# Retention and two feed-forward layers: keys loaded earlier, outputs ahead of scores, weight steps denser

## The chip, the cores and the metric

The kernel runs on one core of a Trainium2 chip. The metric is the device time of one execution in microseconds. TensorE (PE) multiplies matrices, VectorE (DVE) and ScalarE (ACT) do elementwise work and read the results out of PSUM, GpSimd (POOL) does elementwise work in SBUF, and SyncE (SP) issues every transfer, one after the other from one queue.

## The reference

The attention-like part has no softmax: scores are weighted by a decay that depends on the distance of the positions and on the head. Its output, 2304 tokens by 512, goes through two feed-forward layers one after the other, each with its own weights (512 by 2048 and 2048 by 512). All of it is float32.

```python
B, H, S, D = 4, 8, 576, 64
scores = scale * q @ k.transpose(0, 1, 3, 2)
gamma = 1 - 2.0 ** (-5 - arange(H))
ret = scores * where(rel >= 0, gamma ** rel, 0)   # rel = query position - key position
x = (ret @ v) as (B*S, H*D)

h = x @ w_in;  x = maximum(0.01 * h, h) @ w_out   # first layer
h = maximum(x @ w2_in, 0);  out = (h * h) @ w2_out   # second layer
```

## The kernel before

**Retention.** Each batch's 576 positions are cut into four chunks of 128 and one of 64, so there are 20 chunks, counted from 0. For chunk i `load` fetches transposed queries and keys (256 KB each), `load_rows` keys and values by rows (512 KB together), `load_gq` a decay table in the first batch. `scores(i)` forms all heads' scores on TensorE in one of the two big PSUM tiles (a for even, b for odd chunks), and VectorE multiplies them by the decay mask into r (line 513); so the scores of chunk i+2 wait until r of chunk i is done. `decay(i)` scales queries and keys in place on GpSimd (lines 522, 526). `output(i)` multiplies r by the values (line 539), adds the decayed query times the state (line 542), adds this chunk to the state sums (line 548), and ScalarE copies the state (line 554) and the output into ysb (line 557). `keep_warm(n)` issues n products of a zero tile whose result is not used (line 466).

**Weights.** Products run in float32 split into a high and a low part of a format that TensorE takes faster. Weights come from memory in a raw form, 1 MB (two transfers of 512 KB) a task, through a single buffer (the first task through ysb's last tile). A task is a generator of steps: twelve for the first matrix (`steps_in`: lines 149 to 187), eight for the second (`steps_out`: lines 149 and 201 to 216); each step is one to four instructions. Group 0 has four tasks, two of each kind, 40 steps; the sixth step of a second-matrix task, or the seventh of a first-matrix one, asks for the next task's load. During retention that request only sets `free`, and the chunk loop issues the load at its next turn; after retention the load is issued at once, and the task's steps may start only `ARRIVE` units of the planner's clock later. `RATE[i]` says how many steps follow chunk i's output, `OWN` how many of the 40 are left for later, `FIRST` how many run before the loop.

**Operands.** As soon as 768 tokens are out, `operands` builds seven sums and differences of their blocks, each as x with a high part by ScalarE (line 256) and a low part by VectorE (line 260), one step a chunk (`BUILD`). They are stored to memory for later groups (line 237 in the profile).

**Products.** The first matrix is multiplied by a seven-product scheme (`first`), in the order A11, A12, S2, S3, S1, A22, S4. A11, S2, S1 and S4 add into PSUM tile a, A12 into b; S3 starts b anew and A22 adds to it. So t (line 370, from A11 and A12) must have read b before S3, the copy s of S3 (line 344) must be done before A22, and t22 (line 384) must have read a before S4. `second` then multiplies by the second matrix (yps, line 419). There are four groups of weights a layer and three blocks of 768 tokens a group. A11 and A12 of the first block, and S2 behind them, stand among the last two chunks. `pace` runs weight and operand steps between products: at most two weight steps a call, by planned shares. It also issues the stores of x.

Every engine takes its instructions in the order in which the program was written; there is no other scheduler.

Of the kernel before, what the change touches and what calls it, by code (L numbers as in the profile page):

```python
# [23 lines left out]
GRP = 4  # L24
# [6 lines left out]
HW = DM // 2  # L31
SLOTS = 7
INS, OUTS = 3, 2 * NU
RATE = [1, 2, 2, 2] + [2] * 6 + [1, 1, 2, 2, 2, 0, 0, 0, 1, 2]
BUILD = [0] * 8 + [1] * 11 + [0]
DEEP = 4
SPACE = .65
SHARE = {0: (0.15, 0.45), NG - 1: (0.47, 0.85), NG: (0.2, 0.55)}
OWN = 5
LAG = 1  # L40
ARRIVE = 3
FIRST = 3
AHEAD = 2
WARM = 10, 3, 1
BIGGEST = float(np.uint32(0x0FEFFFFF).view(np.float32))

A22, A11, A12, S1, S2, S3, S4 = range(7)
# [3 lines left out]
def retention_ffn_kernel(ctx: ExitStack, tc: tile.TileContext, full, rows, half, halfv, w1, w2, const, mask, gk, out):  # L51
# [54 lines left out]
    class Weights:  # L106
# [30 lines left out]
        def next(self):  # L137

            if self.later:
                self.free = not self.raws  # L140
            else:
                self.ahead()
# [99 lines left out]
    def operands(layer, p):  # L242

        x = ysb[p].rearrange("p (k t n) -> p k t n", k=NK, t=2)
        b11, b21, b12, b22 = (x[:, k : k + 2, t] for t in range(2) for k in (0, 2))
        t2 = stage.tile([P, 2, HT], F32, tag="t2", name="t2")

        xt = {}

        def hi(i, src):  # L250
            use = layer, 0, p, i
            while uses[loaded[0]] != use or loaded[0] == used[0] + SLOTS:
                yield True
            loaded[0] += 1
            xt[i] = xs[use] = xpool.tile([P, 2, 2, HT], F32R, tag="x", name="x")
            nc.scalar.activation(xt[i][:, 0], src, AF.Copy)

        def lo(i, src):
            t = xt[i]
            nc.vector.tensor_tensor(t[:, 1], src, f32(t[:, 0]), sub)  # L260
            kept.append(((layer, 0, p, i), t))


        yield from hi(0, b11)
        yield
        yield from hi(1, b21)
        lo(0, b11)
        yield
        lo(1, b21)
        nc.vector.tensor_tensor(b11, b12, b11, sub)  # L270
        yield
        nc.vector.tensor_tensor(t2, b22, b11, sub)
        yield
        yield from hi(2, t2)
        nc.vector.tensor_tensor(b12, b22, b12, sub)
        yield
        yield from hi(3, b12)
        lo(2, t2)
        yield
        yield from hi(4, b11)  # L280
        nc.vector.tensor_tensor(b21, b21, t2, sub)
        yield
        yield from hi(5, b21)
        lo(3, b12)
        yield
        yield from hi(6, b22)
        lo(4, b11)
        yield
        lo(5, b21)
        yield  # L290
        lo(6, b22)
        yield
# [152 lines left out]
    def tokens(i):  # L445
        b, c = chunks[i]
        return b * S + c * P, P if c < FULL else S - FULL * P
# [112 lines left out]
    weights = Weights()  # L560
# [5 lines left out]
    def run(n, limit):  # L566

        while n > 0 and done[0] < limit:
            if next(steps, None):
                break  # L570
            done[0] += 1
            n -= 1
# [13 lines left out]
    GROUP = NU * (STEPS_IN + STEPS_OUT)  # L586
    with tc.manual_schedule():
        with tc.tile_pool(name="att", bufs=1) as pool:
            att.append(Retention(pool))
            ret = att[0]  # L590
            n = len(chunks)
            ret.load(0)
            ret.load_mask()
            ret.load_rows(0)
            ret.load_gk()
            weights.ahead()
            ret.load(1)
            ret.load_rows(1)
            ret.load_gq(1)
            ret.load(2)  # L600
            ret.load_rows(2)
            ret.load_gq(2)
            ret.load(3)
            ret.load_rows(3)
            ret.load_gq(3)
            ret.keep_warm(WARM[0])
            ret.scores(0)
            ret.decay(0)
            run(FIRST, GROUP)
            scored = 1  # L610
            for i in range(n):
                if i + DEEP < n:
                    ret.load(i + DEEP)
                    ret.load_rows(i + DEEP)
                    if i + DEEP <= FULL:
                        ret.load_gq(i + DEEP)
                if weights.loads < GRP and (weights.free or i == 1):
                    weights.free = False
                    weights.ahead()

                while scored < n and scored <= i + (AHEAD if i > 2 else min(i, 1)):
                    ret.scores(scored)
                    ret.decay(scored)
                    scored += 1
                ret.keep_warm(WARM[i + 1] if i + 1 < len(WARM) else 0)
                ret.output(i)
                a, t = tokens(i)
                if a < 2 * HT <= a + t:
                    builds.append(operands(0, 0))
                run(min(1, RATE[i]), GROUP - OWN)  # L630
                if BUILD[i] > 0:
                    build()
                run(RATE[i] - 1, GROUP - OWN)
                if BUILD[i] > 1:
                    build()
                if i >= n - 3 and i < n - 1:

                    early.append(wide(i - n + 3))
                    product(early[-1], [wt_in[0, 0], wt_in[0, 2]], (A11, A12)[i - n + 3], uses[i - n + 3], True)
                    if i == n - 3:  # L640
                        sums1 = stage.tile([P, NU, HT], F32, tag="t2", name="s")
                        nc.scalar.activation(sums1, early[0][:, :, :HT], AF.Copy)
                    else:
                        early.append(sums1)
        att.clear()
        if weights.free and weights.loads < GRP:
            weights.ahead()
        more = ctx.enter_context(tc.tile_pool(name="more", bufs=1))
        gp = ctx.enter_context(tc.tile_pool(name="gp", bufs=1))
        weight_tiles(more, INS - NU, OUTS - NU)  # L650
        run(GROUP, GROUP - OWN)
        weights.arrive = ARRIVE
        weights.later = False


        whole = NB * 15
        for layer in range(2):
            for g in range(NG):
                i = layer * NG + g


                start = i * GROUP + GROUP
                limit = start + (GROUP if i < 2 * NG - 1 else 0)

                def pace(now, ceiling):

                    into = min(1, (now - 15 * p) / (6 if busy[p] else 12 if p == NB - 1 else 15))
                    share = (0, *SHARE.get(i, (0.36, 0.71)), 1)
                    part = share[p] + (share[p + 1] - share[p]) * into
                    want = start + math.ceil((limit - start) * part)  # L670

                    while len(kept) > LAG:
                        store(*kept.pop(0))
                    while builds and now >= built[0] and build():
                        built[0] = max(built[0], now - 1) + SPACE
                    if not builds:
                        while kept:
                            store(*kept.pop(0))
                    weights.clock = whole * i + now
                    if now % 15 not in (6, 8):  # L680
                        run(min(2, max(want, start if now > 1 else 0) - done[0]), ceiling)

                busy = [g == 0] * (NB - 1) + [layer == 0 and g == NG - 1]
                for p in range(NB):
                    built = [15 * p + 8]
                    if g == 0 and p + 1 < NB:
                        builds.append(operands(layer, p + 1))
                    elif layer == 0 and g == NG - 1 and p == NB - 1:
                        builds.append(operands(1, 0))

                    def in_first(m):
                        if i == p == m == 0:
                            return
                        pace(15 * p + m + 1, max(start, limit - 3))

                    def in_second(t, j, part):

                        if t or j or part in (0.5, 1):
                            pace(15 * p + 7 + 4 * t + 2 * (j + part), limit if p == NB - 1 else max(start, limit - 3))
                        load_x()  # L700

                    gs = first(layer, g, p, in_first)
                    second(layer, g, p, gs, in_second)
                    build(99)
                weights.due = 0
                run(GROUP, limit)
# [56 lines left out]
```

## Time and profile before

| | |
|---|---|
| three runs | 845.59 us median (843.33 to 846.24) |
| profiled execution | 844.29 us, of which the span is 842.50 us |
| mean granted clock of TensorE | 0.993 of full speed |
| TensorE busy | 824.2 us (98%), VectorE 601.4 (71%), ScalarE 340.7 (40%), GpSimd 49.8 (6%) |

The span is what the trace covers, from the first instruction to the last. Times in rows count from its start. Retention takes roughly the first 88 us of it; the rest is the two layers. Engine names in rows: PE, PEld (its weight loads), DVE, ACT, POOL, SPq (SyncE's issue of a transfer).

### The profile page before, as it was taken

To read this page: it belongs to the slowest core of one execution; us is meant where nothing else is said; L and a number is where in the kernel's file an instruction comes from. 1 tells how busy PE (TensorE), PEld (TensorE's weight loads), DVE (VectorE), ACT (ScalarE), POOL (GpSimd) and SP (SyncE) were. 2 spreads that over 40 slices of the span, in tenths; PEclk is the share of its full clock that TensorE was granted. 3 is DMA by queue.
4 is the path that set the end of the run, shared out by engine and by line. 5 is a ranking of instruction groups with operands and counts; after the bars stand their busy time and mean duration, and the time that the engine had idled before them with its cause. 6 is when DMAs were issued, how large, how long until landed. Compare 5 with 4: busy or idle time off the path is not lost.

```text
span 842.5 us, 12378 instructions
## 1 busy us (share of the span) xinstructions
PE 824.2 (98%) x5084; PEld 778.0 (92%) x5084; DVE 601.4 (71%) x734; ACT 340.7 (40%) x447; POOL 49.8 (6%) x36
## 2 busy tenths in 40 slices
PE   6999999999999999999999999999999999999998
PEld 6878899999999999999999998988998998998996
DVE  4799588758667576658667879868777778754534
ACT  1455557545424424424425365543322333321211
POOL 3766000000000000000000000000000000000000
PEclk8999999999999999999999999999999999999999
DMA  9998463967547647646832554966755646735711
GB/s 334 346 311 288 181 241 95 420 264 279 217 190 268 219 150 298 242 147 242 301 112 103 209 226 163 368 255 238 285 183 206 262 160 252 262 133 204 286 52 75
DMA packets 45688, 191.01 MB, mean 227 GB/s; under 512 B 5696, under 2 KB 6720, under 8 KB 45632
## 3 DMA queue, kind: packets, MB, share of 16 engines
q1 hardware_dynamic: 45632, 190.22, 60.7%
q8 instruction: 40, 0.66, 0.3%
q14 instruction: 16, 0.13, 0.0%
HBM read 152.45 MB, written 37.75 MB: 226 GB/s over the span
## 4 chain that ended last, share of the span: by engine, by line
PE 86%; DVE 7%; DMA 4%; ACT 1%; issue 1%; SPq 0%; DVEq 0%; ACTq 0%
PE yps L419 46%; PE a L318 22%; PE b L318 16%; DMA raw<-in_w 1%; DVE r L513 1%; DMA x<-x 1%; DVE x L260 1%; PE scps L511 1%; DMA kt<-in_full 1%; DMA kv<-in_rows 1%; PE ops L539 1%; PE ops L542 1%; DVE sf L205 1%; ACT sf L149 1%; DVE ilo L187 1%
## 5 line engine op out<-in xcount | busy, mean ns | idle before, releaser
L318 PE MATMUL a<-x,ihi 128*128 128x384 f32 x768 | 196.0, 336 | 2.2 <-DVE t L384 2.1
L318 PE MATMUL b<-x,ihi 128*128 128x384 f32 x576 | 147.2, 336 | 2.1 <-DVE t L370 2.1
L318 PEld LDWEIGHTS a<-x,ihi 128*128 128x128 f32 x768 | 138.9, 188 | 4.3 <-DVE t L384 3.4
L419 PE MATMUL yps<-ghi,ohi 128*128 128x384 f32 x384 | 128.6, 335 | 0.6 <-ACT ysb L428 0.6
L318 PE MATMUL a<-x,ilo 128*128 128x384 f32 x384 | 128.6, 335 | 0.0
L419 PE MATMUL yps<-ghi,olo 128*128 128x384 f32 x384 | 128.3, 334 | 0.0
L419 PE MATMUL yps<-glo,ohi 128*128 128x384 f32 x384 | 128.3, 334 | 0.0
L356 DVE TENSOR_TENSOR glo<-t,ghi 128x768 fp32r<-128x768 f32 x96 | 91.7, 955 | 45.8 <-ACT ghi L351 45.3
L430 DVE TENSOR_TENSOR ysb<-yps,ysb 128x384 f32<-128x384 f32 (+1 forms) x126 | 76.0, 610 | 62.6 <-PE yps L419 62.1
L419 PE MATMUL yps<-ohi,glo 128*128 128x512 f32 x288 | 112.3, 390 | 0.0
L419 PE MATMUL yps<-olo,ghi 128*128 128x512 f32 x288 | 112.3, 390 | 0.0
L419 PE MATMUL yps<-ohi,ghi 128*128 128x512 f32 x288 | 112.0, 389 | 0.0
L351 ACT ACTIVATE ghi<-t 128x768 fp32r<-128x768 f32 x96 | 81.1, 845 | 68.5 <-DVE t L329 55.1
L318 PEld LDWEIGHTS b<-x,ihi 128*128 128x128 f32 x576 | 104.3, 189 | 2.6 <-DVE t L370 2.4
L344 ACT ACTIVATE s<-a 128x768 f32<-128x768 f32 x47 | 38.2, 813 | 157.3 <-PE a L318 157.2
L318 PE MATMUL b<-x,ilo 128*128 128x384 f32 x288 | 96.8, 336 | 0.0
L419 PEld LDWEIGHTS yps<-ghi,ohi 128*128 128x128 f32 x384 | 72.1, 188 | 1.5 <-ACT ysb L428 0.9
L318 PEld LDWEIGHTS a<-x,ilo 128*128 128x128 f32 x384 | 72.2, 188 | 0.0
L419 PEld LDWEIGHTS yps<-glo,ohi 128*128 128x128 f32 x384 | 72.1, 188 | 0.0
L419 PEld LDWEIGHTS yps<-ghi,olo 128*128 128x128 f32 x384 | 72.1, 188 | 0.0
L419 PEld LDWEIGHTS yps<-ohi,glo 128*128 128x128 f32 x288 | 54.1, 188 | 11.2
L419 PEld LDWEIGHTS yps<-olo,ghi 128*128 128x128 f32 x288 | 54.1, 188 | 11.0
(67 smaller groups left out, 1002.5 us busy)
## 6 DMA issues: line engine op xcount, KB each, us to landing
x<-x SPq DMA_DIRECT2D x168, 768.0 KB, 6.2
raw<-in_w SPq DMA_DIRECT2D x62, 512.0 KB, 5.1
kv<-in_rows SPq DMA_DIRECT2D x16, 512.0 KB, 6.2
out<-ysb SPq DMA_DIRECT2D x18, 256.0 KB, 2.0
q<-in_full SPq DMA_DIRECT2D x16, 256.0 KB, 5.8
kt<-in_full SPq DMA_DIRECT2D x16, 256.0 KB, 5.6
ysb<-in_w SPq DMA_DIRECT2D x2, 512.0 KB, 7.1
gq<-in_const SPq DMA_DIRECT2D x3, 256.0 KB, 7.3
```

The costliest lines, as they stand in the source:

```text
L149: nc.scalar.activation(f32(a), f32(raw[:, :, 1]), AF.Abs)
L187: nc.vector.tensor_tensor(lo[:, a:z], sf[:, a + 1 : z + 1], f32(hi[:, a:z]), sub)
L205: nc.vector.scalar_tensor_tensor(rest, high, 23, low, ALU.logical_shift_left, ALU.bitwise_or)
L260: nc.vector.tensor_tensor(t[:, 1], src, f32(t[:, 0]), sub)
L318: nc.tensor.matmul(ps[:, u, :HT], a[:, w, s], x[:, b, k], start=(start and k == 0 and i == 0), stop=(k == 1 and i == 2), skip_group_check= ...
L344: nc.scalar.activation(t, ps[:, :, :HT], AF.Copy)
L351: nc.scalar.activation(h, t, AF.Copy)
L356: nc.vector.tensor_tensor(l, t, f32(gs[key][0]), sub)
L419: nc.tensor.matmul(acc, a, b, start=(j == u == i == 0), stop=(j == 1 and u == NU - 1 and i == 2))
L430: nc.vector.tensor_tensor(y, acc, y, add)
L511: nc.tensor.matmul(ps[:n, j, p, :n], k[s, c], q[s, c], start=True, stop=True)
L513: nc.vector.tensor_tensor(t[:n, :, :, :n], ps[:n, :, :, :n], self.mask[:n, :, :, :n], mul)
```

## The change

Chunk 1's queries and keys are loaded ahead of the first weight task. In the loop, `output` of chunks 0, 1 and 2 stands ahead of the next scores instead of behind them. No weight steps run before the loop; the steps per chunk become two, two, then three in chunks 2 to 8, two in 9 to 11, one in 12, none in 13 to 17 and three in 18 and 19, 38 in all with two left for later. The zero products after the first ten are 5 and 4 ahead of the outputs of chunks 1 and 2, where there were 3 and 1 ahead of those of chunks 0 and 1. When retention ends and the buffer is free, the next task is loaded whichever group it belongs to, and since `weights.arrive` is set only afterwards, that task's steps wait for no planned time.

```diff
-RATE = [1, 2, 2, 2] + [2] * 6 + [1, 1, 2, 2, 2, 0, 0, 0, 1, 2]
+RATE = [2] * 2 + [3] * 7 + [2] * 3 + [1] + [0] * 5 + [3, 3]
-OWN = 5
+OWN = 2
-FIRST = 3
-WARM = 10, 3, 1
+WARM = 10, 5, 4
...
+            ret.load(1)
             weights.ahead()
-            ret.load(1)
             ret.load_rows(1)
...
-            run(FIRST, GROUP)
             scored = 1
             for i in range(n):
...
-                while scored < n and scored <= i + (AHEAD if i > 2 else min(i, 1)):
+                if 0 < i < len(WARM):
+                    ret.keep_warm(WARM[i])
+
+                if i < 3:
+                    ret.output(i)
+                while scored < n and scored <= i + (AHEAD if i > 2 else 1):
                     ret.scores(scored)
                     ret.decay(scored)
                     scored += 1
-                ret.keep_warm(WARM[i + 1] if i + 1 < len(WARM) else 0)
-                ret.output(i)
+                if i >= 3:
+                    ret.output(i)
...
         att.clear()
-        if weights.free and weights.loads < GRP:
+        if weights.free:
             weights.ahead()
```

The changed file's lines are numbered one lower than before from the products on (L511 becomes L510, and so on).

TensorE at the start of the program, before (cold is the zero tile, scps scores, ops an output, sums the state sums):

```order
L466 MATMUL cold<-cold 128x128 x10
L511 MATMUL scps<-q,kt 128x128 x8
L466 MATMUL cold<-cold 128x128 x3
L539 MATMUL ops<-r,kv 64x128 x8
L548 MATMUL sums<-kv 64x64 x8
L511 MATMUL scps<-q,kt 128x128 x16
L466 MATMUL cold<-cold 128x128
L539 MATMUL ops<-r,kv 64x128 x8
L542 MATMUL ops<-q,state 128x128 x4
L548 MATMUL sums<-kv 64x64 x8
L511 MATMUL scps<-q,kt 128x128 x8
```

The same place now:

```order
L465 MATMUL cold<-cold 128x128 x10
L510 MATMUL scps<-q,kt 128x128 x8
L538 MATMUL ops<-r,kv 64x128 x8
L547 MATMUL sums<-kv 64x64 x8
L510 MATMUL scps<-q,kt 128x128 x8
L465 MATMUL cold<-cold 128x128 x5
L538 MATMUL ops<-r,kv 64x128 x8
L541 MATMUL ops<-q,state 128x128 x4
L547 MATMUL sums<-kv 64x64 x8
L510 MATMUL scps<-q,kt 128x128 x8
L465 MATMUL cold<-cold 128x128 x4
```

Before, the scores of chunks 1 and 2 (x16) stood ahead of chunk 1's output; now each output stands ahead of the next scores, and it is the scores of chunk 2 that come behind chunk 1's whole output.

VectorE where retention ends and the first products are summed, before (r is the last chunk's; the first L214 and the L216 belong to the third weight task, L201 to L209 and the second L214 to the fourth; t is the sum of A11 and A12, glo the low part of the first activations):

```order
L513 TENSOR_TENSOR r<-scps,mask 64x8x64
L260 TENSOR_TENSOR x<-ysb_66,x 128x768
L214 TENSOR_SCALAR sf<-sf 128x1024
L260 TENSOR_TENSOR x<-ysb_66,x 128x768
L216 SCALAR_TENSOR_TENSOR olo<-sf 128x1024
L201 TENSOR_SCALAR raw<-raw 128x1024
L203 TENSOR_SCALAR sf<-sf 128x1024
L205 SCALAR_TENSOR_TENSOR sf<-raw 128x1024
L370 TENSOR_TENSOR t<-b,s 128x768
L207 TENSOR_SCALAR sf<-sf 128x1024
L209 SCALAR_TENSOR_TENSOR sf<-raw,sf 128x1024
L214 TENSOR_SCALAR sf<-sf 128x1024
```

The same place now, to t22 (the last row; L158 to L162 belong to the fifth task):

```order
L202 TENSOR_SCALAR sf<-sf 128x1024
L204 SCALAR_TENSOR_TENSOR sf<-raw 128x1024
L206 TENSOR_SCALAR sf<-sf 128x1024
L208 SCALAR_TENSOR_TENSOR sf<-raw,sf 128x1024
L369 TENSOR_TENSOR t<-b,s 128x768
L213 TENSOR_SCALAR sf<-sf 128x1024
L215 SCALAR_TENSOR_TENSOR olo<-sf 128x1024
L158 TENSOR_SCALAR sf<-sf 128x1024
L355 TENSOR_TENSOR glo<-t,ghi 128x768
L160 TENSOR_SCALAR sf<-sf 128x1024
L162 SCALAR_TENSOR_TENSOR sf<-raw,sf 128x1024
L383 TENSOR_TENSOR t<-a,s 128x768
```

Four instructions of the fourth task stand ahead of t instead of two, and three of the fifth task stand between t and t22, where the rest of the fourth stood.

ScalarE at the same place, before (ysb_68 are the outputs of the last two chunks, L149 the fourth task's first step, L642 and L344 copies of products):

```order
L557 ACTIVATE ysb_68<-ops 128x4x128
L557 ACTIVATE ysb_68<-ops 128x4x64
L149 ACTIVATE sf<-raw 128x1024
L327 ACTIVATE t<-t 128x768
L344 ACTIVATE s<-a 128x768
L351 ACTIVATE ghi<-t 128x768
L212 ACTIVATE ohi<-sf 128x1024
L344 ACTIVATE s<-b 128x768
```

And now (the first L148 is the fourth task's first step, the second the fifth's):

```order
L556 ACTIVATE ysb_68<-ops 128x4x128
L148 ACTIVATE sf<-raw 128x1024
L556 ACTIVATE ysb_68<-ops 128x4x64
L211 ACTIVATE ohi<-sf 128x1024
L326 ACTIVATE t<-t 128x768
L343 ACTIVATE s<-a 128x768
L350 ACTIVATE ghi<-t 128x768
L148 ACTIVATE sf<-raw 128x1024
L343 ACTIVATE s<-b 128x768
```

The fourth task's first step has moved ahead of the last chunk's copy, and the fifth task's first step has come in ahead of the copy of S3 (s<-b). In SyncE's queue the fifth task's load now stands ahead of the first six stores of x, where it stood behind them.

## Rows read from the trace of the kernel before

**Rows 1.** Stretches: length; PE, PEld, DVE, ACT, POOL busy; granted clock, DMA share, GB/s
```profile
15.65:22.00 6.35, 6.35 (x42) 5.46 (x42) 6.32 (x5) 0.00 (x0) 4.67 (x4) 0.53 1.07 363
...
92.50:97.00 4.50, 4.50 (x17) 4.50 (x18) 2.99 (x4) 4.03 (x5) 0.00 (x0) 0.62 0.33 100
...
150.00:842.00 692.00, 686.86 (x3683) 650.48 (x3681) 483.86 (x611) 263.20 (x322) 0.00 (x0) 1.00 0.59 220
```

**Rows 2.** Timeline, 13 to 24 us: start, length, engine, instruction [idle before, releaser]
```profile
14.34 1.76 POOL L522 TENSOR_TENSOR q<-q,gq 128x512 f32<-128x512 f32 x1 [4.57 <-DMA gq<-in_const]
15.65 2.08 PE L511 MATMUL scps<-q,kt 64*128 64x128 f32 x16 [2.12 <-DMA kt<-in_full]
18.05 1.27 POOL L522 TENSOR_TENSOR q<-q,gq 128x512 f32<-128x512 f32 x1
23.84 1.23 DVE L513 TENSOR_TENSOR r<-scps,mask 128x1024 f32<-128x1024 f32 x1 [1.70 <-PE scps L511]
```

**Rows 3.** Timeline, TensorE, outputs of chunks 2 and 3
```profile
24.74 1.16 PE L542 MATMUL ops<-q,state 128*128 128x128 f32 x8
25.83 0.69 PE L548 MATMUL sums<-kv 128*64 128x64 f32 x16
...
28.15 1.09 PE L539 MATMUL ops<-r,kv 128*64 128x128 f32 x16
```

**Rows 4.** Waits of VectorE, 23.84 to 74.27: total us, times, longest
```profile
DVE r L513 <- PE scps L511: 3.1, 2, 1.7
DVE sf L159 <- ACT sf L149: 1.4, 1, 1.4
DVE ilo L187 <- ACT ihi L185: 0.8, 1, 0.8
```

**Rows 5.** Timeline, VectorE behind r of chunk 17; TensorE, scores of chunk 19
```profile
74.27 1.89 DVE L260 TENSOR_TENSOR x<-ysb,x 128x768 fp32r<-128x768 f32 x1
...
75.92 0.68 PE L511 MATMUL scps<-q,kt 64*64 64x64 f32 x16
```

**Rows 6.** Waits of TensorE, 23.84 to 92.6
```profile
PE scps L511 <- DVE r L513: 2.2, 4, 0.9
```

**Rows 7.** VectorE's groups, 23.8 to 79.8, then 84 to 140: busy us, mean ns
```profile
L260 DVE TENSOR_TENSOR x<-ysb,x 128x768 fp32r<-128x768 f32 x5 | 7.9, 1590 | 0.0
...
L260 DVE TENSOR_TENSOR x<-ysb,x 128x768 fp32r<-128x768 f32 x7 | 6.4, 951 | 0.0
```

**Rows 8.** Timeline, 85 to 97: ScalarE, VectorE, TensorE around t
```profile
85.26 0.60 ACT L557 ACTIVATE ysb<-ops 128x512 f32<-128x512 f32 x1
...
88.60 1.12 ACT L149 ACTIVATE sf<-raw 128x1024 f32<-128x1024 f32 x1
...
89.75 0.69 DVE L203 TENSOR_SCALAR sf<-sf 128x1024 f32<-128x1024 f32 x1 [5.16 <-ACT sf L149]
...
90.36 1.22 DVE L205 SCALAR_TENSOR_TENSOR sf<-raw 128x1024 uint32<-128x1024 uint32 x1
...
91.50 0.95 DVE L370 TENSOR_TENSOR t<-b,s 128x768 f32<-128x768 f32 x1
...
92.50 0.61 PE L318 MATMUL b<-x,ihi 128*128 128x384 f32 x2 [2.08 <-DVE t L370]
...
96.07 0.81 ACT L344 ACTIVATE s<-b 128x768 f32<-128x768 f32 x1 [0.32 <-PE b L318]
```

**Rows 9.** Chain of waits from S3 (b) on: start, length, what
```profile
92.50 3.53 PE b L318 x12
...
98.50 2.08 PE b L318 x12
...
102.66 16.64 PE yps L419 x96
```

**Rows 10.** Raw weights' tile, the fifth task's load: issue ns min/median/max, its times; landing
```profile
L132 SPq DMA_DIRECT2D raw<-in_w x2: 333/380/426, 94.4 to 94.8; - x2
...
DMA to landing us min/median/max: 4.3/5.1/5.9
```

## The prediction

> **What bounds the kernel now.** I read the share of each engine over long stretches first [rows 1]: from 150 us to the end TensorE is busy 686.86 of 692 us, so nothing the change touches can pay there, and any shift of the moment at which TensorE enters the steady part is a shift of the end. That moment is the first product of the second matrix, at 102.66 us in the chain of waits [rows 9]. Everything below is how this mark moves. Before it lie three stretches. Up to about 24 us the input loads and VectorE's and GpSimd's first work set the pace, and TensorE runs at half clock for 6 us (granted 0.53 between 15.65 and 22) after a stretch in which it mostly waited for keys and for decayed queries [rows 1, 2]. From 24 to about 76 us VectorE is the narrow engine: between the start of the fourth chunk's masked scores (r at 23.84) and the end of the eighteenth's (74.27) it idles only 3.1 - 1.7 + 1.4 + 0.8 = 3.6 us of 50.4 [rows 2, 4, 5], and TensorE waits for r four times, 2.2 us together [rows 6]. From 76 us TensorE works through the last chunks and the first products until 90.4, and then waits 2.08 us for t, the sum of the first two products: t stands on VectorE behind two instructions of the fourth weight task, whose first step waits on ScalarE behind the copy of the last chunk's output [rows 8]. After that wait TensorE runs at half clock again (0.62 over 92.5 to 97): twelve products take 3.53 us where the same form later takes 2.08 [rows 1, 9].
>
> **The change part by part.** Chunks are counted from 0, r3 is the fourth chunk's r; X is how much earlier than before TensorE starts the scores of chunk 19 (75.92 [rows 5]).
>
> *Start.* Chunk 1's keys go in front of the first weights' 1 MB, so its scores need not wait for them, but what comes next is new: chunk 1's output now stands ahead of chunk 2's scores on TensorE. That output needs the decayed query and key, and GpSimd can begin the first only at 14.34, when its factors land [rows 2]; they stand in the queue behind as many bytes as before. From there: two GpSimd instructions of 1.27 to 16.9, state sums 0.69 to 17.6, scores 1.16 to 18.7, r2 1.23 to 20.0, output of chunk 2 1.09 + 1.16 + 0.69 to 22.9, scores of chunk 3 1.16: r3 starts at 24.1, against 23.84 [rows 2, 3]. Chunk 2's scores, which before ran at 15.65 beside the wait, give up their place: that eats what the earlier keys bring. The nine cold products lie in the waits and are costed at nothing; if the half clock falls on them and on the output, as on the scores at 15.65 (2.08 for 1.16), r3 comes about 1.4 us later. The bounds are 23 and 25.5.
>
> *Middle.* VectorE has done three weight instructions before r3 where it had done five, and it has all seven of the third task behind it by r17, where two came later. So between r3 and the end of r17 it has four instructions more: two of 0.69 and two of 1.22, 3.8 us [rows 8]. Without idle time the stretch takes 50.4 - 3.6 + 3.8 = 50.6 us. The weight instructions now stand closer together while GpSimd works, and the two slow each other: five instructions that form x average 1590 ns there, and seven after 84 us, when GpSimd is all but done, 951 [rows 7]. I add 1.2 us for that, a third of the 3.8 by that ratio. Then r17 ends at 24.1 + 50.6 + 1.2 = 75.9. The scores of chunk 19 wait for r17's buffer; before, they came at 75.92 with r17 ready at 74.27. X = 0: the denser steps turn the slack of 1.6 us into a tie. TensorE's own chain would allow more. With r3 at 24.1, the output of chunk 3 could start at 24.1 + 1.23 + 1.16 = 26.5 instead of 28.15 [rows 3], 1.6 us, and the waits for r are 2.2: X is at most 3.8. Three weight loads wait in SyncE's queue for VectorE, and two now come two or three chunks earlier in it; TensorE, late by VectorE's measure, covers the chunk loads behind them, so I take 0, and up to 1 us if that cover fails.
>
> The Trainium skill has a rule here that speaks against the change ("SBUF — State Buffer", section "Who interferes with whom"): VectorE and GpSimd share a pair of ports under an exclusive lock, and an instruction with two SBUF inputs blocks on it. The 1590 against 951 ns agrees. By the strict rule no weight step can hide GpSimd's work, and my 1.2 us would be nearer 3, an estimate.
>
> *End.* Two things change. First, the fourth task is further on: its first step now stands on ScalarE in front of the last chunk's copy, behind that of chunk 18, which ends at 85.86 [rows 8]. From there 1.12 on ScalarE to 86.98, then four VectorE steps of 0.61, 1.14, 0.61 and 1.14 from start to start to 90.5, then t, 0.95: TensorE goes on at 91.5 - X where it did at 92.50, a wait of 1.1 us in place of 2.08. Second, the fifth task (group 1's first weights) is loaded at once, and its steps start without the planner's delay. Its buffer is the one that the fourth task reads until 90.5. SyncE issues at once after such a release, the second half 0.4 later, and it lands 5.9 after that, as the same load did before at 94.4 and 94.8 [rows 10]: 96.9. On ScalarE the task's first step (1.12) now stands in front of the copy of product S3 (0.81), and that copy must be over before A22 is added into the same PSUM tile: A22 can start at 98.9 - X. TensorE itself gets there at 91.5 + 2 x 2.08 = 95.7, so it waits 3.2 us for a load that nobody needs yet. Before, that copy ran at 96.07 and A22 stood in the chain at 98.50 [rows 8, 9]. A wait that is longer than the 2.08 us of before should bring the half clock again: A22 3.53, to 102.4, then S4, 2.08 and some 0.2 if the half clock reaches into it: 104.7. VectorE is not later: the task's second step, glo, two steps and the sum t22 take about 0.61 + 0.95 + 0.61 + 1.14 + 0.95 from 98.0, to 102.3. So the mark stands at 104.7 - X against 102.66, +2.0 us.
>
> On that load the skill gives another price ("DMA: Bandwidth & Descriptors", section "Anatomy of one DMA — SWDGE (gpsimd) path"): 2.0 us plus the bytes at 436 GB/s, 4.4 us for both halves, an estimate. It is stated for another issuing path, and the row of before has 6.3. By it A22 would start at 97.0 and the mark move by about -0.2.
>
> *Costed at nothing:* the stores of x, which now follow that load 15 us later than before; a tile of x is written anew only once the second matrix's products have begun, 12 us later, and ScalarE has time there. If that cover fails, 1 us on ScalarE, not on TensorE. From the fifth task's sixth step on, the order of every engine is as before.
>
> **The sum.** +2.0 - X with X = 0: +2.0 us. The profiled execution took 844.29 us (842.50 of span and 1.79 around it), so 846.3; the median shown is 845.59, 1.3 above that execution, and on it the forecast is 847.6.
>
> **The rivals.**
> - *The load is hidden.* If the fifth task's data lands by the time S3 ends, TensorE goes through: 91.5 + 4 x 2.08 = 99.8, -2.8 us, 842.8. For it: the queue is nearly empty there. Against it: the release and the 6.3 us are read from rows, and the place on ScalarE from the order. Chance 0.12.
> - *VectorE is not the limit in the middle* (less collision with GpSimd, or r3 at 23). Then X lies between 1.2 and 3.8, and the end at -1.8 to +0.8, middle 845.1. For it: 3.6 us of idle time to use up and four waits to lose. Chance 0.23.
> - *Slower: the collisions with GpSimd decide.* Between 24 and 76 us VectorE stands without a break, and GpSimd's 23 or so instructions find it busy. If six more weight steps than before are stretched as x was, by 0.64 each, that is 3.8 us, 2.6 beyond the 1.2 taken: X = -2.6, the end at +4.6, 850.2. It decides from the point where TensorE's waits for r pass 5 us. For it: the x instructions of rows 7. Against it: the 46.8 us that VectorE was not idle in rows 4 and 5 hold such collisions already. Chance 0.14.
> - *The change does no more than shuffle:* start and middle cancel and the load lands 1 to 2 us earlier than its row: about +0.3, 845.9. Chance 0.08.
>
> **How the numbers follow.** The forecast has the remaining 0.43, from 846.6 to 848.8 (X between -1.2 and 1.0). A measurement of this kernel can tell about 0.3%, 2.5 us, from no change: faster is below 843.0, slower above 848.1. Slower: all of the third rival and about half of the forecast's own spread, since 847.6 lies only 0.5 below the line, 0.36 in all. Faster: the first rival and the end of the second, 0.16. The rest, 0.48, is no change. The range leaves out most of the first rival and the upper part of the third: 843.2 to 850.4.
>
> **What would show it.** Right: r3 close to 24.1; VectorE idle under 1.5 us from r3 to r17; more wait for r than 2.2 us, most of it in chunks 8 to 16; a wait before S3 near 1.1 us; a wait of about 3 us before A22, whose releaser is the copy of S3 behind the fifth task's first step; the mark at 104 to 105. Wrong: no wait at A22, or a scores start for chunk 19 before 74 or after 77.5.

## Result, and the profile after: slower by 9 us

The changed kernel takes 853.98 us (median of four runs, 852.06 to 857.68), the kernel before 844.93 (four runs): a ratio of 1.012, 95% interval 1.0097 to 1.0143. The forecast was 847.6 with a range up to 850.4, so the time lies outside it. The four runs are two at 852.1 and 852.4 and two at 855.6 and 857.7; the profiled execution is the one of 855.57 us (span 853.8), 11.3 above the profiled one of before.

The mark of the prediction, the first product of the second matrix, lies at 114.14 us instead of 102.66: +11.48, the whole difference of the spans (11.3). The steady part behind it is as full as before; see the last row. Stretches, with length, busy time of PE, PEld, DVE, ACT and POOL, granted clock, DMA share and GB/s; they answer to [rows 1]:

```profile
9.82:14.60 4.78, 4.78 (x49) 4.44 (x49) 0.00 (x0) 1.86 (x4) 1.04 (x1) 0.50 1.04 413
...
42.08:46.00 3.92, 3.92 (x46) 3.49 (x48) 3.85 (x5) 1.89 (x5) 0.67 (x2) 0.62 0.43 135
70.55:75.22 4.67, 4.67 (x41) 4.15 (x41) 4.67 (x6) 1.87 (x4) 0.00 (x0) 0.66 0.94 338
108.16:112.00 3.84, 3.84 (x13) 3.67 (x14) 3.81 (x5) 0.23 (x1) 0.00 (x0) 0.59 1.02 427
150.00:853.00 703.00, 698.24 (x3749) 661.76 (x3747) 495.45 (x623) 271.33 (x335) 0.00 (x0) 1.00 0.59 220
```

TensorE is granted half its clock (1.2 of 2.4 GHz) in four places, each of them behind a wait of 2.6 to 3.1 us; before there were two.

The waits of TensorE from the fourth chunk's r (25.57) to the mark, which answer to [rows 6], and those of VectorE from 25.57 to 81, which answer to [rows 4] (total us, times, longest):

```profile
PE scps L510 <- DVE r L512: 6.6, 6, 2.6
PE b L317 <- ACT s L343: 3.1, 1, 3.1
PE ops L541 <- ACT state L553: 2.6, 1, 2.6
PE b L317 <- DVE t L369: 1.1, 1, 1.1
PE scps L510 <- DMA kt<-in_full: 0.7, 1, 0.7
```

```profile
DVE r L512 <- PE scps L510: 2.4, 3, 1.4
DVE ilo L186 <- ACT ihi L184: 0.9, 1, 0.9
```

TensorE's waits for r have tripled, from 2.2 us to 6.6, and three waits are new. VectorE's 1.4 stands ahead of r3; behind it VectorE idles twice for 0.5.

The middle, timeline of VectorE and TensorE, which answers to [rows 5]. The r rows are those of the thirteenth, fourteenth and eighteenth chunk (12, 13 and 17 counted from 0), the scores those of chunks 14, 15 and 19; L204 and L208 belong to the third weight task:

```profile
61.09 2.29 DVE L204 SCALAR_TENSOR_TENSOR sf<-raw 128x1024 uint32<-128x1024 uint32 x1
63.30 1.21 DVE L512 TENSOR_TENSOR r<-scps,mask 128x1024 f32<-128x1024 f32 x1
64.56 0.68 PE L510 MATMUL scps<-q,kt 64*64 64x64 f32 x16 [1.77 <-DVE r L512]
...
67.30 2.06 DVE L208 SCALAR_TENSOR_TENSOR sf<-raw,sf 128x1024 uint32<-128x1024 uint32 x1
69.28 1.21 DVE L512 TENSOR_TENSOR r<-scps,mask 128x1024 f32<-128x1024 f32 x1
70.55 2.08 PE L510 MATMUL scps<-q,kt 64*128 64x128 f32 x16 [2.58 <-DVE r L512]
...
79.78 1.22 DVE L512 TENSOR_TENSOR r<-scps,mask 128x1024 f32<-128x1024 f32 x1 [0.54 <-PE scps L510]
...
84.97 0.68 PE L510 MATMUL scps<-q,kt 64*64 64x64 f32 x16
```

Chunk 19's scores start at 84.97 where they started at 75.92: X is -9.05. They no longer wait for r17, which is over at 81.0; from 70.55 on it is VectorE that waits for TensorE. Chunk 15's scores, at 70.55 here, stood 8.8 us earlier in the kernel before:

```profile
61.72 1.16 PE L511 MATMUL scps<-q,kt 64*128 64x128 f32 x16 [0.86 <-DVE r L513]
```

The end, ScalarE, VectorE and TensorE around t, which answers to [rows 8] (the L148 is the fifth task's first step):

```profile
99.58 0.95 DVE L369 TENSOR_TENSOR t<-b,s 128x768 f32<-128x768 f32 x1
100.58 0.62 PE L317 MATMUL b<-x,ihi 128*128 128x384 f32 x2 [1.10 <-DVE t L369]
...
106.28 1.12 ACT L148 ACTIVATE sf<-raw 128x1024 f32<-128x1024 f32 x1 [3.37 <-DMA raw<-in_w]
107.30 0.80 ACT L343 ACTIVATE s<-b 128x768 f32<-128x768 f32 x1
108.16 1.01 PE L317 MATMUL b<-x,ihi 128*128 128x384 f32 x2 [3.12 <-ACT s L343]
```

And the chain of waits behind it (start, length, what), which answers to [rows 9, 10]:

```profile
100.11 6.07 DMA raw<-in_w
106.18 0.02 issue
106.20 0.04 ACTq L148
106.24 0.04 issue
106.28 1.12 ACT sf L148
107.41 0.71 ACT s L343
108.11 0.04 issue
108.16 3.77 PE b L317 x12
111.93 2.21 PE a L317 x12
114.14 16.64 PE yps L418 x96
```

From chunk 19's scores to the mark it is 29.17 us where it was 26.74: +2.43. The load, the step on ScalarE, the copy and A22 at half clock stand in the chain one behind the other, as forecast.

### The profile page after: what moved, and what is told of

The parts are those of the page before. It is cut to its first block, busy times and chain, and to the rows that moved or that the text cites. A ratio compares the mean times of both kernels' runs of the same rounds, so it can differ in the third digit from the quotient of the medians.

```text
span 853.8 us, 12396 instructions
## 1 busy us (share of the span) xinstructions
PE 828.8 (97%) x5094; PEld 781.9 (92%) x5094; DVE 603.3 (71%) x734; ACT 340.8 (40%) x447; POOL 49.8 (6%) x36
## 4 chain that ended last, share of the span: by engine, by line
PE 88%; DVE 5%; DMA 3%; ACT 2%; issue 1%; SPq 0%; POOL 0%; ACTq 0%; DVEq 0%; POOLq 0%
PE yps L418 46%; PE a L317 21%; PE b L317 16%; DMA raw<-in_w 2%; PE scps L510 2%; PE ops L538 2%; PE ops L541 1%; DVE r L512 1%; PE sums L547 1%; DMA mask<-in_mask 1%; ACT sf L148 1%; DVE sf L204 1%; DVE sf L208 1%; DVE sf L202 0%; DMA kv<-in_rows 0%
## 5 line engine op out<-in xcount | busy, mean ns | idle before, releaser
L418 PEld LDWEIGHTS yps<-ohi,glo 128*128 128x128 f32 x288 | 54.0, 188 | 11.3
L369 DVE TENSOR_TENSOR t<-b,s 128x768 f32<-128x768 f32 x24 | 23.0, 957 | 58.6 <-PE b L317 58.5
```

The lines of the kernel that those rows point to most:

```text
L369: nc.vector.tensor_tensor(t11, b[:, :, :HT], s1, add)
L418: nc.tensor.matmul(acc, a, b, start=(j == u == i == 0), stop=(j == 1 and u == NU - 1 and i == 2))
```

## Experiments

Times are medians; the ratio is to the kernel before on the same chip, with its 95% interval. The median of before lay between 844.3 and 844.9 in all five sessions. "Held" means a planner time that keeps the fifth task's steps behind the first products.

**One part at a time.** Four kernels: the change with the fifth task's steps held; then, each in the kernel before, chunk 1's keys ahead alone, the order of outputs and scores alone, and the steps with the unconditional load alone.

```diff
# the change, held
         if weights.free:
             weights.ahead()
+            weights.due = 8
# before, steps alone
-RATE = [1, 2, 2, 2] + [2] * 6 + [1, 1, 2, 2, 2, 0, 0, 0, 1, 2]
+RATE = [2] * 2 + [3] * 7 + [2] * 3 + [1] + [0] * 5 + [3, 3]
-OWN = 5
+OWN = 2
-            run(FIRST, GROUP)
-        if weights.free and weights.loads < GRP:
+        if weights.free:
```

> The changed kernel, only the fifth weight task's steps held until the first block's seven products are done (the load itself is still issued at once). Theory: the wait of 3.1 us before A22 and the half clock behind it (A22 3.77 instead of 2.08) are that task's first step on ScalarE, so both go: the first product of the second matrix moves from 114.1 to 109 to 109.5 us, the time falls by 4.5 to 5 us, to about 849. Rival: something else holds A22 (VectorE's t22, the stores of x), then under 1.5 us come back.

> The kernel before, only chunk 1's keys loaded ahead of the first weights. Both theories (dense steps cost the time; or the new order at the start does): chunk 1's scores come 2 us earlier, chunk 2's still wait for their keys at about 15.65, so no change: -0.5 to +0.5 us. Rival: the half clock around 15 to 22 us goes with the shorter wait, then -1.5 to -2.5 us.

> The kernel before, only chunks 0 to 2's outputs ahead of the next scores, with 5 and 4 zero products. Theory dense steps: r3 starts 1 to 2 us later than 23.84 and most of it is absorbed by VectorE's idle time, +0.5 to +2 us. Rival theory start: the late r3 is carried through all chunks and the half clock with it, +4 us or more.

> The kernel before, only the weight steps changed (the new table, two left for later, none before the loop, the fifth task loaded at once). Theory dense steps: the end costs 2.4 us, and in the middle r12 and r13 come late and ScalarE holds chunk 5's state, 4 to 7 us: +6.5 to +9 us, the scores of chunk 19 at 81 to 84. Rival theory start: only the end, +2 to +3.5 us, chunk 19's scores at 76 to 77.

Measured: held 847.35 (845.84 to 849.08), ratio 1.0031 (1.002 to 1.0041); keys 844.72, 1.0011 (0.9996 to 1.0025); order 843.61, 0.9997 (0.9982 to 1.0013); steps 852.04, 1.0091 (1.0068 to 1.0114). Each edit of the start alone is worth nothing that can be told from zero; for the order 0.5 to 2 us more had been expected. The steps with their load are most of the loss, 7.8 of 9 us; chunk 19's scores come at 81.65 there. Holding the fifth task gives back 6.6 of the change's 9 us, and the two traces show 4.9 of it. The load itself is still issued at once there (at 96.42), and only its first step stands later on ScalarE, at 109.51: the wait before A22 is gone, and from chunk 19's scores (81.66) to the mark (105.89) it is 24.23 us instead of 29.17. The mark lies earlier than the 109 to 109.5 expected, because chunk 19's scores also came 3.3 us earlier in this execution. So it is the step in front of the copy that costs, not the load's traffic. What is left of held against before, 3 us, hides a larger loss: its end is 2.5 us shorter than that of before, its scores of chunk 19 are 5.7 us later.

**What the middle costs, and through whom.** Held with two steps a chunk; held without GpSimd's scaling of queries and keys, which is left out for all chunks but the first (the output is then another one); and the same left out in before.

```diff
# held, flat
-RATE = [2] * 2 + [3] * 7 + [2] * 3 + [1] + [0] * 5 + [3, 3]
+RATE = [2] * 14 + [1] * 4 + [3, 3]
# held, and before: no scaling in the loop
                     ret.scores(scored)
-                    ret.decay(scored)
```

> The changed kernel with the fifth task held, and the same 38 steps spread flat: two a chunk to chunk 13, one in 14 to 17, three in the last two, so that the end is as in the run with the fifth task held. Theory dense steps (three a chunk in chunks 2 to 8 make VectorE late for the scores of chunks 11 to 15, and TensorE then has the rest of its own chain still before it): chunk 19's scores go from 81.7 back to 75 to 77.5 and the time falls by 4 to 6 us against 847.4, to 841.5 to 843.5, under the kernel before. Rival (38 steps are too many wherever they stand): chunk 19's scores stay at 80 to 82, the time within 1.5 us of 847.4.

> The changed kernel with the fifth task held, without GpSimd's scaling of queries and keys (decay is left out for all chunks but the first). Theory dense steps with collisions (VectorE's weight steps and GpSimd slow each other, some 10 us between 24 and 70): without GpSimd chunk 19's scores come at 73 to 77 instead of 81.7, the time falls by 4 to 7 us more than the same cut brings the kernel before. Rival (late weight loads and ScalarE's steps in front of the state, no collisions): chunk 19's scores stay at 79 or later.

> The kernel before without GpSimd's scaling of queries and keys (left out for all chunks but the first): the base for the same cut in the changed kernel. Expected by both theories: chunk 19's scores at 73 to 75.5 instead of 75.9 (waits for r and GpSimd of 3 us go, half clock stays), the time down by 0.5 to 2.5 us.

Measured: flat 843.16, ratio 0.9979 (0.9969 to 0.9988); held without scaling 840.78, 0.9963 (0.9944 to 0.9981); before without scaling 841.41, 0.9968 (0.9951 to 0.9985). Without GpSimd's work the dense kernel loses nothing against before: 3 us of difference have become -0.6. The cut was worth 3.1 us in before, a little more than expected, and 6.6 in held. Chunk 19's scores start at 73.93 in the one and 74.10 in the other. The one flat execution that has a trace is the slowest of its eleven, 849.0, and chunk 19's scores stand at 82.82 in it, not at the 75 to 77.5 expected; what the flat steps do to the middle is known by their time alone. The groups of the third task's two long instructions (busy us, mean ns), in the changed kernel and then in held without scaling:

```profile
L204 DVE SCALAR_TENSOR_TENSOR sf<-raw 128x1024 uint32<-128x1024 uint32 x1 | 2.3, 2285 | 0.0
L208 DVE SCALAR_TENSOR_TENSOR sf<-raw,sf 128x1024 uint32<-128x1024 uint32 x1 | 2.1, 2060 | 0.0
```

```profile
L208 DVE SCALAR_TENSOR_TENSOR sf<-raw,sf 128x1024 uint32<-128x1024 uint32 x1 | 1.2, 1219 | 0.0
L204 DVE SCALAR_TENSOR_TENSOR sf<-raw 128x1024 uint32<-128x1024 uint32 x1 | 1.2, 1218 | 0.0
```

The same instruction takes 2285 ns beside GpSimd's work and 1218 without.

**Is it the queue of loads?** Held, with the third and fourth weight loads one chunk later in SyncE's queue, behind the loads of the chunk.

```diff
-                if weights.loads < GRP and (weights.free or i == 1):
-                    weights.free = False
+                if weights.loads < GRP and (late or i == 1):
+                    weights.free = late = False
                     weights.ahead()
+                else:
+                    late = weights.free
```

> The changed kernel with the fifth task's steps held (847.35) and, besides, the third and fourth weight loads issued one chunk later in SyncE's queue, behind the chunk loads that now follow them. Theory (VectorE's steps, stretched by GpSimd, make the loss in the middle): those waits for r stay, only the wait for the keys at chunk 12 (0.50 us) goes, so within 0.5 us of 847.35: 846.8 to 847.6. Rival (weight loads issued earlier push the keys of the chunks back, and that is the loss): the earlier loads cost what the held version loses to before, some 3 us, so 844 to 845.5.

Measured: 847.58, ratio 1.0039 (1.0022 to 1.0055), as held. The wait for chunk 12's keys went, and a wait for keys of 3.0 us stood near the start of that profile; the time did not move. The queue is not the loss.

**Which steps of the middle?** Two kernels, both as dense as the change up to chunk 8 and held. In the first the third task's remaining seven steps are moved from chunks 9 to 12 to chunks 14 to 17; in the second they run at the flat version's times, most in chunks 12 to 15, one a chunk but for chunk 13.

```diff
-RATE = [2] * 2 + [3] * 7 + [2] * 3 + [1] + [0] * 5 + [3, 3]
+RATE = [2] * 2 + [3] * 7 + [0] * 5 + [2, 2, 2, 1, 3, 3]
# the second
+RATE = [2] * 2 + [3] * 7 + [0] * 3 + [1, 2] + [1] * 4 + [3, 3]
```

> The changed kernel with the fifth task's steps held (847.35), as dense as that up to chunk 8, but the third task's remaining seven steps moved from chunks 9 to 12 to chunks 14 to 17. Theory (what counts is VectorE's work up to the fourteenth chunk's r, since TensorE needs 13 to 14 us from chunk 15's scores to chunk 19's in every run): the steps of the third task leave that stretch, chunk 15's scores come 4 to 6 us earlier than 68.71, of which 1 to 2 are given back as waits for r behind them; 842 to 844.5. Rival (the density in chunks 2 to 8 is what costs): 846 to 847.5.

> Three steps a chunk in chunks 2 to 8 as in the changed kernel, none in 9 to 11, and from chunk 12 on exactly as many steps done as in the flat version (843.16): it differs from that in chunks 2 to 11 alone. If the place of the third task (chunks 9 to 12) is what costs, 842.5 to 844. If the density in chunks 2 to 8 costs by itself, 846 to 848. With the fifth task's steps held, as there.

Measured: the first 847.16 (843.62 to 850.31), ratio 1.0032 (1.0016 to 1.0048); the second 842.91, 0.999 (0.9971 to 1.0009). The first missed: its profile does show chunk 15's scores at 62.85 instead of 68.71, but then L204 and L208 run beside GpSimd again, at 2290 and 1745 ns, and the product A11 waits 1.8 us for r and runs partly at half clock. Part of the gain is given back there: that execution took 844.96, 2.2 us less than the median, and no slower one has a trace. The second separates them: three steps a chunk early on cost nothing that can be told from the flat version; the place of the third task does. There the two long instructions took 1.20 us each, and the timeline of GpSimd and VectorE shows why:

```profile
60.55 1.44 POOL L521 TENSOR_TENSOR q<-q,gq 128x256 f32<-128x256 f32 x1
61.95 1.04 POOL L525 TENSOR_TENSOR kv<-kv,gk 128x512 f32<-128x512 f32 x1
66.92 1.20 DVE L204 SCALAR_TENSOR_TENSOR sf<-raw 128x1024 uint32<-128x1024 uint32 x1
68.22 2.52 POOL L521 TENSOR_TENSOR q<-q,gq 128x512 f32<-128x512 f32 x1 [5.23 <-PE scps L510]
70.66 1.20 DVE L208 SCALAR_TENSOR_TENSOR sf<-raw,sf 128x1024 uint32<-128x1024 uint32 x1
70.71 2.94 POOL L525 TENSOR_TENSOR kv<-kv,gk 128x512 f32<-128x512 f32 x1
```

GpSimd rests 5 us behind chunk 14, and L204 falls into that rest; when GpSimd comes back behind a busy VectorE it is GpSimd that is stretched (2.52 and 2.94 us for forms that take 1.27 and 1.75 a few rows later), and GpSimd has time. In before the third task stands in the same place, and its L205 keeps its 1.20 us beside a GpSimd instruction of 4.37:

```profile
66.85 4.37 POOL L522 TENSOR_TENSOR q<-q,gq 128x512 f32<-128x512 f32 x1 [5.41 <-PE scps L511]
67.40 1.20 DVE L205 SCALAR_TENSOR_TENSOR sf<-raw 128x1024 uint32<-128x1024 uint32 x1
```

In the changed kernel GpSimd is at work around it, from 53.7 to 68.3 with one rest of 1.1, and VectorE loses.

**A version that beats both.** In before, the wait of 2.08 us ahead of S3 goes if no weight steps follow the last two chunks. The same tail was added to the start's two edits, and to the flat version.

```diff
-RATE = [1, 2, 2, 2] + [2] * 6 + [1, 1, 2, 2, 2, 0, 0, 0, 1, 2]
+RATE = [1, 2, 2, 2] + [2] * 6 + [1, 1, 2, 2, 2, 0, 0, 0, 0, 0]
-OWN = 5
+OWN = 8
```

> The kernel before with no weight steps in the last two chunks (eight left for later instead of five), so that t, the sum of the first two products, stands on VectorE ahead of the whole fourth task. From the rows of the wait of 2.08 us before S3 and of the half clock behind it (3.53 for 2.08): both go, the first product of the second matrix moves from 102.66 to 99 to 100, the time falls by 2.5 to 3.7 us. Rival: the four steps come back as waits for the second matrix's weights or for t22, then under 1 us.

> Before's steps, with both parts of the start taken over (chunk 1's keys ahead, the first three outputs ahead of the next scores) and no weight steps behind the last two chunks, OWN 8. Theory (the start is neutral and the tail is worth 3 us by itself): 841.4, between 840.5 and 842. Rival (the start gains something that the wait at the end hid): 839 to 840.5. If the start costs something that was hidden: over 842.3.

> The flat version (two steps a chunk, 843.16) with no weight steps behind the last two chunks and OWN 8, so that t stands ahead of the whole fourth task. Theory (what is left in the flat version is the wait of 1.1 us before S3): 843.2 less 1.1 and a little VectorE time, 841.2 to 842.4. Rival (six steps more in the steady part delay the next weights there): 843.2 or above.

Measured: the tail in before 841.41, ratio 0.9967 (0.9955 to 0.9978); with the start's edits 843.75, 0.9992 (0.9975 to 1.0009), a miss by 2 us; flat with the tail 842.15, 0.9976 (0.9961 to 0.9991). In the first, t starts at 89.54, beside the copy of the last chunk's output, TensorE doesn't wait for it, A22 runs at full clock, and the first product of the second matrix starts at 99.98 (102.50 in before by the same row). In the profile of the second, chunk 2's scores start only at 21.93, and TensorE waits 7.3 us for r ahead of outputs, 4.4 of it in one piece. The order of outputs and scores alone, with the same early steps, cost nothing that can be told from zero, so why the two edits seem to give up part of the tail's gain stays open. The tail in before has the lowest median measured here of a version that computes everything; its interval overlaps with that of the flat version with the tail.

## Why the prediction was wrong

**The end was right.** Forecast: a wait of 1.1 us before S3, then 3.2 before A22 with the copy of S3 behind the fifth task's first step as its cause, A22 at 3.53, and +2.0 at the mark. Measured: 1.10, 3.12 with that releaser, 3.77 and +2.43. The load took 6.07 us to land from its second half's issue, as the 5.9 of [rows 10] said; the rival that hides it fell. The held version showed the part of that step on ScalarE.

**The start lay just beyond its upper bound.** r3 came at 25.57, forecast 24.1, bounds 23 to 25.5. The first output waited for a mask that landed late, the half clock fell on it, on the state sums and on chunk 1's scores, and GpSimd began its first decayed query at 15.70 where the forecast had 14.34:

```profile
8.49 1.23 DVE L512 TENSOR_TENSOR r<-scps,mask 128x1024 f32<-128x1024 f32 x1 [6.95 <-DMA mask<-in_mask]
9.82 1.98 PE L538 MATMUL ops<-r,kv 128*64 128x128 f32 x16 [3.09 <-DVE r L512]
15.70 1.27 POOL L521 TENSOR_TENSOR q<-q,gq 128x512 f32<-128x512 f32 x1 [4.65 <-DMA kv<-in_rows]
16.93 1.49 POOL L525 TENSOR_TENSOR kv<-kv,gk 128x512 f32<-128x512 f32 x1
18.53 0.69 PE L547 MATMUL sums<-kv 128*64 128x64 f32 x16
```

The delay is 1.47 us, and the text had priced a half clock at 1.4. That the two agree is luck: the state sums at 18.53 need the keys that GpSimd finished at 18.42, so a full clock alone would have brought them hardly earlier. In the six experiments with the same start and with GpSimd's work r3 came at 23.40 to 24.65, so the forecast of 24.1 was sound and this execution a late one.

**The middle is the step that failed.** It summed VectorE's work from r3 to the end of r17, counted four instructions more, and set chunk 19's scores by r17's buffer: X = 0. Measured is X = -9.05, in three pieces. 1.47 is the start. 3.6 is VectorE: from r3 to the end of r17 it took 81.0 - 25.57 = 55.4 us, forecast 51.8. Of that 1.9 is idle time, which the sum had put at nothing, and 1.7 is stretch beyond the 1.2. The last 4.0 (84.97 - 81.0) lie behind r17, where the text had no term at all.

The count of four was right up to r17, and r17 was the wrong place to count. Between r3 and r13 VectorE has eight weight instructions more than before (26 against 18), because the six that before stand between r13 and r17 have become two. These eight take 0.72 + 1.95 + 1.33 + 1.53 + 0.68 + 2.29 + 0.68 + 2.06 = 11.2 us, where their counterparts take 7.6 in the kernel before. Idle time gave 2.7 back (3.6 to 0.9), the other instructions 1.4: r3 to r13 grew from 36.62 to 43.71 us. Only then come the last chunks, and there TensorE has its own length: from chunk 15's scores to chunk 19's it is 14.4 us in the changed kernel (1.5 of it half clock: 2.08 and 1.65 for 1.16 and 1.09), 14.2 in before, where it waits, and 12.95 to 13.06 in seven experiments in which it didn't wait there. VectorE's lighter end had nothing to give: it idles behind r13 while TensorE, 8.8 us late at 70.55, passes the whole delay on.

The third rival, collisions with GpSimd, named part of the mechanism and had 0.14; its sign, waits for r past 5 us, came true (6.6), but its price, 2.6 us beyond the 1.2, also ended at r17. The 1.2 itself was read wrongly off its rows: 1590 against 951 ns is two thirds more, not one, and on 3.8 us that is 2.5. Stretch measured to r17 is 2.9 (55.4 less 46.8 of work before, 3.8 for the four and 1.9 idle).

How much of the 7 us up to r13 is count and how much GpSimd? The weight instructions between r3 and r13 add up to 19.0 us in before (18 of them) and 13.3 in before without scaling; to 29.5 in the changed kernel (26), 28.2 in held, and 21.0 in held without scaling. So the eight more are 7.7 us by themselves, GpSimd stretched the 18 by 5.7 already in before, and it stretches the 26 by 7.2 in held and by 8.5 in the changed kernel. The collisions grew by 1.5 to 2.8 only. What the experiments show is that the loss needs both: without GpSimd's work the dense steps fit, and VectorE even idles 3.8 us in that stretch; with it they don't, and moving the third task behind r13, partly into GpSimd's rest, takes the loss away again. That last move also takes work out of the stretch, so it doesn't part the two.

The Trainium skill's rule ("SBUF — State Buffer", section "Who interferes with whom"), quoted in the prediction as the one that speaks against the change, would have been the nearer price: its 3, an estimate, stands against 2.9. What the runs show besides is that either engine can be the one that is stretched.

**Not costed, and not nothing in the profile.** ScalarE's first step of the second task waited for the buffer sf, which VectorE read until 40.1, and held a state copy back; TensorE then waited 2.59 us and ran at half clock from 42 to 46:

```profile
37.17 2.93 DVE L186 TENSOR_TENSOR ilo<-sf,ihi 128x768 fp32r<-128x768 f32 x2
40.13 1.14 ACT L148 ACTIVATE sf<-raw 128x1024 f32<-128x1024 f32 x1 [2.93 <-DMA kv<-in_rows]
41.18 0.76 ACT L553 ACTIVATE state<-sums 64x256 f32<-64x256 f32 x2
42.08 1.20 PE L541 MATMUL ops<-q,state 128*128 128x128 f32 x8 [2.59 <-ACT state L553]
```

The load named as releaser in the second row is of kv, which this step doesn't read; it starts as the instruction above it ends, at 40.10. Where a later task's first step waited in the same way (2.17 us at 54.10 in the second kernel of the pair on the third task), the profile names that VectorE instruction. The profile of held has no such wait. Nor has that of the steps alone, at 852.15, where the longest wait for a state is 0.2 us. Whether it is what parts the two runs above 855 from the two at 852 is open: only one of them has a trace.

Of the tests that the prediction set itself, the waits before S3 and A22 and the growth of the waits for r came out; r3, VectorE's idle time (1.9 us from r3 to r17, forecast under 1.5) and the mark did not, and "chunk 19's scores after 77.5", which was named there as what would make it wrong, is what happened.

## What to carry to other kernels

When two engines take turns as the limit, count the moved work at the last point where the first one is waited for, not at the end of the stretch: what it saves afterwards can't be handed back once the second engine runs its own chain. Work on VectorE beside GpSimd is priced by what GpSimd does at that very time, so put long steps where GpSimd rests, and leave slack, since the loser can change from run to run. And a step that needs a load must not stand on an in-order engine in front of a copy that the next product waits for.

## What the runs showed of the hardware

- VectorE and GpSimd stretch each other, and which one loses depends on the moment: L204 took 2285 ns in the changed kernel with GpSimd at work before it, and its counterpart L205 1204 in before while GpSimd's instruction at 66.85 took 4.37 us. With the same steps in the same place the other one lost in the trace of chunk 1's keys alone (847.33, median 844.72): GpSimd's instruction at 67.19 kept its 1.28 us, L205 took 1.68, L260 behind it 1.80 and L207 1.75, and chunk 19's scores came at 78.79 instead of 75.92. A price per instruction that is read from one place doesn't hold in another.
- The length of a wait alone doesn't tell whether the half clock follows. A wait of 2.58 us for r was followed by it (0.66 over 70.55 to 75.22), one of 1.77 at 64.56 was not: the scores there took 0.68 us, the full-clock time of that form. But with the steps alone a wait of 1.87 at 53.55 was followed by half clock (0.50 over 53.55 to 56), and in held without scaling one of 2.81 at 30.65 was not (1.00 over 30.65 to 33).
